# An attention recurrence and a feed-forward layer on one core: every on-chip transpose moved from the DMA crossbar to TensorE, in a newly searched order

## The chip, the core and the metric

The kernel runs on one core of a Trainium2 chip. A core has a matrix engine (TensorE, PE in the profile; its weight loads are listed apart as PEld), a vector engine (VectorE, DVE), a scalar engine (ScalarE, ACT), a general engine (GpSimd, POOL) and a queue engine (SyncE, SP) that here issues nearly all DMAs. Each engine takes its instructions strictly in the order in which the program gives them; engines wait for each other by semaphores. The metric is device microseconds (us) of one launch, median of several.

## What is computed

An RWKV-like linear attention over 768 steps, then a feed-forward layer with a squared ReLU:

```python
for t in range(S):                        # B, H, S, D = 4, 8, 768, 48
    cur = einsum('bhd,bhe->bhde', u * kt, vt)
    y[:, :, t] = einsum('bhd,bhde->bhe', rt, state + cur)
    state = wt[..., None] * state + einsum('bhd,bhe->bhde', kt, vt)
x = y.transpose(0, 2, 1, 3).reshape(3072, 384)
r = maximum(x @ w_in, 0)                  # w_in 384 x 2048
out = (s * r * r + b) @ w_out             # w_out 2048 x 384
```

## The kernel before

The recurrence is done in chunks of 128 steps: 6 chunks for each of 4 batches, 24 chunk-batches, numbered n = 0 to 23. The first four (`n < PK`, PK = 4) are handled as two interleaved pairs ("packed"). For one chunk-batch all 8 heads stand side by side, 384 numbers for each of 128 time steps. Its steps, by the names that the order uses:

- `load`: w, r, k, v come in by four DMAs (192 KB each); `ln`, `cum`, `exp`, `inc`, `exn`: the logarithm of w, its running sum (a matmul with a triangle), and the two exponentials E.
- `mul` (L482, L489, DVE): R and K times E give `prd`, bf16, two heads to a 128-wide block padded to 64 each: 8 blocks.
- `tr` (L538, TensorE): 8 matmuls against an identity turn the 8 blocks of `prd` into PSUM; `tev` (ACT L552 or DVE L554, by a mark in the order) copies them to the tile `RK`. For a chunk-batch that `xbar_rk(n)` names, `tev` is one DMA instead (L575, `dtrans`): the crossbar of the DMA turns `prd` into `RK`, with no `tr`.
- `mt` (L605, L617): 16 matmuls on `RK` for each chunk-batch, always two chunk-batches together; `msk` (L629, DVE): the masks; `ymm` (L667, L676): y from the state and from the masked products; `rkp`, `rku`, `yd`, `st` (POOL L346, L352, L375, L793) and `cd` (DVE): the diagonal term and the new state; `dmm`, `sup`: the state's increment.
- `yev` (L758): y goes to `x_sb`. `xtr` (L804, TensorE): 3 matmuls against an identity turn it, and `xev` (L552 or L554) copies that to `xT`. Where `xbar_x(n)` holds, `xev` is one crossbar DMA (L585, `dxtr`), with no `xtr`.

The feed-forward layer takes tiles T = 0 to 11 of two chunk-batches (256 rows). For each there are eight `g1` steps (L858: 6 matmuls of 128x256 each, into one PSUM bank), a `relu` (ACT L871) and a `sq` (square; ACT L881 or DVE L883) after each, then eight `g2` steps (L901: 4 matmuls of 128x384 each), `oev` (L912, DVE) and `store`. The weights are loaded and cast in five pieces (`li`/`lo`, `ci`/`co`).

What runs when is neither a loop nor a scheduler's choice at build time: the string `ORDER` lists all steps, one word each, and the kernel emits their instructions in that order; `@A`, `@D`, `@P` put a movable step on ACT, DVE or POOL, and `+3` emits three matmuls on a zero tile (L1286), which only fill TensorE. Since every engine takes its instructions in program order, the order of the words is the order on each engine and on SP's queue. The `Plan` that checks the words also holds the buffer rings: 6 PSUM banks of tag `P` and 2 of tag `o`, 4 `RK` tiles, 4 `rh` tiles. The costs and due times that its steps carry play no part when the kernel is built from the string.

The choice of the transposing unit is in these constants and lines:

```python
DTK = 9
DTX = 18
    def xbar_rk(n):
        return n >= DTK or (n >= DK2 and n % 2 == 1)
    def xbar_x(n):
        return n >= DTX or (n >= DX2 and n % 2 == 1)
```

So before the change 9 chunk-batches have R and K turned by TensorE and 15 by the crossbar, and 18 have x turned by TensorE and 6 by the crossbar.

Of the kernel before, what the change touches and what calls it, by code (L numbers as in the profile page):

```python
# [42 lines left out]
rkp0 mul0.0 load2.1 cum1.1 mul0.1 exp1.1 rkp1 load4.0 u_ev@D tr0 mul1.0 +4 tev0@A mul1.1 rku1 li0
tr1 load2.3 exl0 +2 rku0 cd1 tev1@A li1 ln2 cd0 mt0 load4.1 msk1.0 cum2.0 rkp3 l21 li2 msk0.0 +2 yd1
ln4 exp2.0 cum3.0 cum3.1 msk0.1 l20 rku3 ci0@A load4.2 msk1.1 cum4.0 +3 vb0@D vb1@A yd0 mul2.0
exp2.1 lo0 dmm0 exp3.1 mul2.1 +2 li3 exp3.0 li4 exl2 mul3.0 exp4.0 l23 cum4.1 sup0 vb3@P ymm0.0
exp4.1 tr2 rkp2 ci1@A mul3.1 st0 ymm0.1 sup1 ydm0 vb2@A l24 lo1 rku2 ymi0 yev0@D tr3 yev1@A tev2@D
xtr0 tev3@A xtr1 l22 +1 st1 xev0@D cd2 xev1@A mt2 cd3 rkp4 ci2@A g10.0 msk3.0 yd3 g10.1 msk2.0
relu0.0 lo2 msk2.1 yd2 ymm2.0 relu0.1 g10.2 msk3.1 rku4 dmm2 mul4 relu0.2 ymm2.1 ydm2 co0@A ci3@P
g10.3 sq0.1@A sup2 yev2@A cd4 st2 ymi2 sq0.2@A xtr2 sup3 yev3@A csred0@D lo3 g10.4 sq0.0@A ci4@D  # L50
load5.0 xev2@A xtr3 g10.5 load6.0 relu0.3 co1@D xev3@A lo4 g10.6 csred1@D sq0.3@A load5.1 g11.0
relu0.6 csadd1@D g11.1 relu0.4 co2@D relu0.5 g20.0 csred2@D sq0.4@A g10.7 sq0.6@A g11.2 sq0.5@A
relu0.7 g11.3 csadd2@D relu1.0 load5.2 g20.1 co3@D relu1.3 g20.4 relu1.1 load6.1 csred3@D ln5 g20.5
ln6 tr4 sq0.7@A cum6.0 csadd3@P tev4@D cum5.0 relu1.2 g11.4 inc6 sq1.3@A load6.2 g11.5 sq1.0@A co4@D
cum5.1 exp5.0 g11.6 small2 csred4@D exp5.1 load5.3 exp6.0 g20.6 exn6 g11.7 relu1.6 mul5 relu1.4
small g20.7 sq1.1@A load4.3 csadd4@D g20.2 relu1.7 load7.0 cssplit tr5 sq1.2@A load8.0 relu1.5 mul6
csspread g20.3 csevac load8.1 tev5@D vb5@P tr6 sq1.5@A rkp5 oev0.0 tev6@A mt4 load9.0 oev0.1 g21.4
l25 msk4.0 sq1.4@A rku5 load7.1 dmm5 g21.0 vb4@A msk5.0 g21.5 ln7 load7.2 sup5 rkp6 sq1.7@A msk4.1
cum7.0 st5 yd4 dmm4 load8.2 g21.1 load9.1 ln8 exp7.0 sup4 l26 cum8.0 cd5 st4 ymm4 ln9 msk5.1 yd5
g21.6 sq1.6@A inc7 load6.3 ymm5 exp8.0 st3 yev4 cum9.0 exn7 g21.7 yev5 rku6 inc8 xtr4 xtr5 g21.2  # L60
xev4@A load10.0 mul7 l27 xev5@A g21.3 exn8 load9.2 inc9 rkp7 g12.0 oev1.1 exp9.0 load9.3 g12.1 mul8
relu2.0 l28 relu2.1 load7.3 g12.2 cd6 l29 sq2.1@A sq2.0@D yd6 g12.3 load11.0 tr7 load10.1 exn9
oev1.0 relu2.2 g12.4 tev7@D vb6@P relu2.3 load8.3 g12.5 relu2.4 sq2.3@D mul9 sq2.4@A mt6 relu2.5
g22.4 msk7.0 store0.0 sq2.2@A vb7@P g12.6 msk6.0 sq2.5@A rkp9 load11.1 tev9 msk6.1 dmm6 g22.0
relu2.6 rku7 ln10 sup6 g12.7 load10.2 ln11 msk7.1 tr8 rku9 relu2.7 cd7 g22.1 sq2.7@A cum10.0 cd9
tev8@A load12.1 vb9@A dmm7 ymm6 rkp8 inc10 g22.5 rku8 yev6 load12.0 cum11.0 sup7 g22.6 yd9 xtr6
inc11 exp11.0 exp10.0 g22.2 yd7 xev6@A cd8 load15.0 ymm7 sq2.6@A vb8@P mt8 yev7 exn11 load13.0 st6
g22.3 exn10 msk8.0 st7 store0.1 xtr7 g22.7 xev7@D load11.2 msk8.1 rkp10 dmm9 load10.3 g13.0 store1.1
msk9.0 l210 g13.1 rku10 msk9.1 relu3.0 load11.3 g13.2 sq3.0@A sup9 yd8 mul10 g13.3 relu3.2 load12.2
st9 g13.4 ln12 relu3.1 g13.5 oev2.0 sq3.1@A ymm9 oev2.1 relu3.3 dmm8 g13.6 mul11 rkp11 relu3.4 rku11  # L70
sq3.3@A g13.7 load14.0 load13.1 sq3.2@A g23.0 sup8 relu3.5 g23.4 yev9 relu3.6 sq3.4@D l211 tev11
load13.2 sq3.5@A ymm8 cum12.0 relu3.7 yev8 xtr9 vb11@P g23.1 st8 ln13 inc12 tev10 xtr8 sq3.7@D g23.5
xev8@A exp12.0 g23.6 xev9@D store1.0 exn12 vb10@D load12.3 sq3.6@D cum13.0 ln14 dmm11 mul12 g14.0
exp13.0 ln15 g14.1 inc13 tev12 cd10 g23.2 exn13 cd11 load14.1 relu4.1 yd10 dmm10 g14.2 sup10 rkp13
g23.3 sup11 relu4.2 load14.2 mul13 g14.3 sq4.1@A rkp12 relu4.0 g14.4 oev3.0 relu4.3 tev13 mt10
sq4.0@A rku13 g23.7 relu4.4 load15.1 msk10.0 sq4.3@A g14.5 msk10.1 l213 sq4.2@A l212 rku12 msk11.0
cum14.0 g14.6 relu4.5 msk11.1 load13.3 exp14.0 st10 cum15.0 exp15.0 g14.7 oev3.1 vb12@A ymm11 inc15
load17.0 relu4.7 yd11 ymm10 sq4.4@D sq4.5@A g24.4 store2.0 st11 relu4.6 sq4.7@A g24.0 cd12 load16.0
inc14 load15.2 exn14 sq4.6@A rkp14 g24.5 yd12 cd13 mt12 yev10 load16.1 vb13@A rku14 yev11 g24.1
msk12.0 g24.6 msk12.1 store2.1 xtr10 xtr11 load19.1 msk13.0 g24.2 xev10@A xev11@A msk13.1 dmm12 ln16  # L80
g24.7 exn15 cd14 load16.2 g15.0 rkp15 mul14 g15.1 relu5.0 l215 g15.2 relu5.1 load19.2 sup12 g15.3
sq5.0@A mul15 dmm13 st12 relu5.2 ymm12 g24.3 relu5.3 load14.3 sup13 sq5.3@A oev4.1 g15.4 rku15
sq5.2@A yev12 g15.5 ln17 tev15 sq5.1@D yd13 tev14 relu5.4 ymm13 g15.6 oev4.0 cd15 load15.3 st13
cum17.0 relu5.6 xtr12 g15.7 xev12@D relu5.5 rkp16 yev13 g25.4 sq5.4@A load17.1 inc17 sq5.6@A l214
load18.0 g25.0 cum16.0 rku16 relu5.7 inc16 store3.0 xtr13 vb14@A rkp19 g25.5 xev13@D store3.1
exp17.0 exp16.0 g25.1 load17.2 l217 sq5.5@A rku19 load18.1 g16.0 load17.3 dmm14 yd15 g16.1 relu6.0
sup14 exn16 cd16 yd14 relu6.1 mt14 exn17 g25.6 msk14.0 load19.0 vb15@A g16.2 msk14.1 sq5.7@A
load16.3 mul16 g16.3 rkp17 sq6.0@A relu6.2 g16.4 msk15.0 g25.2 msk15.1 sq6.1@A relu6.3 load18.2
rku17 ln18 g16.5 sq6.3@A mul17 g16.6 tev16 st14 sq6.2@A dmm15 relu6.6 load20.3 cum18.0 ymm14 sup15
relu6.4 g25.7 cd19 l216 tev17 relu6.5 g25.3 vb16@P oev5.1 ln19 st15 g16.7 oev5.0 load20.0 rkp18  # L90
ymm15 exp18.0 vb17@D relu6.7 g26.0 yev14 sq6.4@A load21.0 inc18 rku18 cum19.0 xtr14 yev15 exn18
g26.4 inc19 xev14@A l218 g26.5 store4.1 sq6.5@A load22.0 sq6.7@A xtr15 dmm17 g26.1 load20.1 xev15@D
exp19.0 mul18 sq6.6@A g17.0 load18.3 exn19 sup17 dmm16 g17.1 relu7.0 sup16 cd17 g17.2 relu7.1
sq7.0@D g17.3 mul19 relu7.2 yd17 load19.3 g17.4 ln20 st17 relu7.3 mt16 load21.1 sq7.3@A g26.2
msk17.0 relu7.4 load20.2 ln21 st16 g26.3 msk16.0 sq7.2@A g17.5 msk17.1 yd16 store4.0 sq7.1@A
load21.2 msk16.1 cum21.0 g26.6 vb18@P tev19 oev6.0 ln22 l219 g17.6 vb19@P relu7.5 sq7.4@D inc21
store5.1 yd19 ymm17 relu7.6 tev18 ymm16 cum20.0 g27.4 yev16 rkp20 exp20.0 load23.0 yev17 exp21.0
g27.5 exn21 inc20 rku20 xtr16 sq7.5@D xtr17 g26.7 xev16@A load21.3 exn20 rkp21 dmm19 xev17@D g17.7
cd18 g18.0 sup19 relu7.7 rku21 mul20 store5.0 g18.1 sq7.7@A vb20@P yd18 cum22.0 g27.6 relu8.0 g18.2
oev6.1 tev20 exp22.0 mul21 relu8.1 load22.1 g18.3 sq7.6@A supn20 load22.2 relu8.2 g18.4 relu8.3  # L100
g27.0 inc22 sq8.0@A supn21 dmm18 cd20 mt18 sq8.1@D tev21 sup18 g27.7 relu8.4 msk19.0 sq8.3@A
load23.1 g27.1 msk18.0 ln23 g27.2 exn22 msk18.1 sq8.4@A g18.5 oev7.1 ymm18 rkp22 vb21@D sq8.2@A
g27.3 yev18 cum23.0 msk19.1 st18 xev18 g18.6 exp23.0 oev7.0 store6.0 yd20 g28.0 load23.2 inc23
relu8.6 ymm19 rku22 cd21 exn23 g18.7 relu8.5 g28.4 mul22 yd21 g28.5 relu8.7 sq8.5@A yev19 supn22
sq8.6@A mt20 sq8.7@D xev19 g28.1 load22.3 msk21.0 rkp23 load23.3 g28.6 msk20.0 tev22 g28.2 msk20.1
rku23 msk21.1 g28.7 st19 store6.1 mul23 g28.3 store7.1 ymm20 g19.0 cd22 supn23 tev23 ymm21 vb22@D
relu9.0 yd22 g19.1 yev20 sq9.0@A yev21 g19.2 xev20 relu9.1 sq9.1@A cd23 g19.3 oev8.1 yd23 g19.4
oev8.0 relu9.3 g19.5 store8.0 relu9.4 store8.1 g19.6 relu9.2 sq9.4@A g29.4 sq9.2@D relu9.5 xev21
g19.7 vb23@D sq9.3@A store7.0 sq9.5@A mt22 relu9.7 g29.5 msk22.0 relu9.6 g29.6 msk22.1 sq9.6@A g29.0
sq9.7@D msk23.0 g29.7 ymm22 g110.0 yev22 g110.1 msk23.1 xev22 oev9.1 g110.2 relu10.1 store9.1 g110.3  # L110
# [1216 lines left out]
```

## Time and profile before

| what | value |
|---|---|
| median of 3 runs | 183.34 us (183.16 to 183.92) |
| the profiled execution: its time | 183.5 us |
| its span, first to last instruction | 181.7 us |
| granted TensorE clock | 1.000 |
| DVE busy | 142.8 us (79%), 257 instructions |
| ACT busy | 142.2 us (78%), 279 instructions |
| POOL busy | 105.0 us (58%), 139 instructions |
| DMA queue of SP | 116,528 packets, 34.42 MB, 81.6% of 16 engines |
| crossbar DMAs `RK<-prd` | 15, 3.7 us from issue to landing |
| crossbar DMAs `xT<-x_sb` | 6, 2.6 us from issue to landing |

Busy is time in which an engine had at least one instruction running. Matmuls overlap in the pipeline, so the mean length of one (220 ns for a transposing matmul) is not the time by which it delays the next; that is seen from how many finish in a stretch. The chain of waits follows, from the last instruction backwards, what released each step, and lists stretches in order of time. The windows give busy time per engine in stretches of the span.

### The profile page before, as it was taken

To read this page: it belongs to the slowest core of one execution; us is meant where nothing else is said; L and a number is where in the kernel's file an instruction comes from. 1 tells how busy PE (TensorE), PEld (TensorE's weight loads), DVE (VectorE), ACT (ScalarE), POOL (GpSimd) and SP (SyncE) were. 2 spreads that over 40 slices of the span, in tenths; PEclk is the share of its full clock that TensorE was granted. 3 is DMA by queue.
4 is the path that set the end of the run, shared out by engine and by line. 5 is a ranking of instruction groups with operands and counts; after the bars stand their busy time and mean duration, and the time that the engine had idled before them with its cause. 6 is when DMAs were issued, how large, how long until landed. Compare 5 with 4: busy or idle time off the path is not lost.

```text
span 181.7 us, 4868 instructions
## 1 busy us (share of the span) xinstructions
PE 171.8 (95%) x1874; PEld 131.9 (73%) x1876; DVE 142.8 (79%) x257; ACT 142.2 (78%) x279; POOL 105.0 (58%) x139
## 2 busy tenths in 40 slices
...
GB/s 154 323 324 343 387 350 274 260 184 206 167 207 178 187 187 182 199 171 183 232 186 195 212 172 202 208 199 243 160 206 100 158 238 153 69 60 11 0 43 132
DMA packets 116554, 34.72 MB, mean 191 GB/s; under 512 B 110898, under 2 KB 114739, under 8 KB 116531
## 3 DMA queue, kind: packets, MB, share of 16 engines
q1 hardware_dynamic: 116528, 34.42, 81.6%
...
q10 hardware_dynamic: 2, 0.00, 0.0%
...
## 4 chain that ended last, share of the span: by engine, by line
PE 64%; DVE 10%; DMA 7%; POOL 6%; issue 5%; ACT 4%; SPq 1%; DVEq 0%; ACTq 0%; POOLq 0%
PE o_ps L901 27%; PE h_ps L858 26%; DMA wo_st<-in_moe_w_out_dram 4%; DMA rkt<-in_k_dram 3%; PE mt_ps L617 2%; POOL rkp L346 2%; PE y_ps L676 2%; DVE prd L489 2%; PE y_ps L667 2%; POOL rku L352 1%; POOL yd L375 1%; PE d_ps L741 1%; ACT rh L871 1%; PE cums L410 1%; PE xt_ps L804 1%
## 5 line engine op out<-in xcount | busy, mean ns | idle before, releaser
L901 PE MATMUL o_ps<-w_out,gT 128*128 128x384 bf16 (+2 forms) x400 | 71.8, 320 | 0.5 <-ACT gT L881 0.5
L858 PE MATMUL h_ps<-xT,w_in 128*128 128x256 bf16 x576 | 70.9, 273 | 1.1 <-POOL w_in L983 0.6
L871 ACT ACTIVATE rh<-h_ps 128x512 bf16<-128x512 f32 x96 | 54.4, 597 | 16.6 <-PE h_ps L858 15.7
L858 PEld LDWEIGHTS <-w_in 128*128 128x128 bf16 x576 | 59.9, 110 | 6.1 <-issue 1.0
L901 PEld LDWEIGHTS <-gT 128*128 128x128 bf16 x400 | 36.1, 98 | 19.7 <-ACT gT L881 0.7
L881 ACT ACTIVATE gT<-rh 128x512 bf16<-128x512 bf16 x78 | 47.4, 634 | 0.5
L352 POOL TENSOR_TENSOR rku<-rkp,u_bc 128x384 f32<-128x384 f32 x24 | 27.7, 1158 | 2.2 <-DVE cd L369 1.6
L346 POOL TENSOR_TENSOR rkp<-rkt 128x384 f32<-128x384 f32 x20 | 21.3, 1068 | 11.2 <-DMA rkt<-in_k_dram 9.4
L629 DVE TENSOR_TENSOR mt_sb<-mt_ps,tri_strict 128x512 bf16<-128x512 f32 x40 | 25.4, 681 | 1.9 <-PE mt_ps L617 1.8
L375 POOL TENSOR_TENSOR yd<-vt,cd 128x384 bf16<-128x384 f32 x20 | 17.6, 884 | 11.0 <-DVE cd L369 10.7
L489 DVE TENSOR_TENSOR prd<-rkt,E 128x768 bf16<-128x768 f32 x20 | 23.7, 1187 | 0.3 <-ACT E L473 0.3
L912 DVE SCALAR_TENSOR_TENSOR o_sb<-o_ps,s_bc,bconst 128x384 f32<-128x384 f32 (+2 forms) x25 | 14.6, 594 | 6.4 <-PE o_ps L901 6.3
L883 DVE TENSOR_TENSOR gT<-rh 128x512 bf16<-128x512 bf16 x18 | 9.6, 536 | 10.2 <-ACT rh L871 10.2
L793 POOL TENSOR_TENSOR st<-stmp,l 128x384 bf16<-128x384 bf16 x16 | 15.5, 972 | 0.8 <-DVE stmp L784 0.8
L758 DVE TENSOR_TENSOR x_sb<-y_ps,yd 128x384 bf16<-128x384 f32 x20 | 10.7, 549 | 5.3 <-PE y_ps L676 5.2
L369 DVE TENSOR_REDUCE cd<-rku 128x8 f32<-128x384 f32 x24 | 12.8, 542 | 1.4 <-POOL rku L352 1.4
L448 ACT ACTIVATE E<-cums 128x388 f32<-128x388 f32 (+1 forms) x22 | 10.4, 496 | 4.3 <-DVE inc L463 2.4
L784 DVE TENSOR_TENSOR stmp<-d_ps,st 128x384 bf16<-128x384 f32 x16 | 8.7, 550 | 3.2 <-PE d_ps L741 3.1
L473 ACT ACTIVATE E<-inc 128x384 f32<-128x384 f32 x18 | 9.3, 525 | 1.5 <-DVE inc L463 1.4
L1286 PE MATMUL warm_ps<-warm_sb 128*128 128x512 bf16 x22 | 7.7, 477 | 1.3 <-DVE warm_sb L1242 1.2
L983 POOL CAST vb<-vt 128x384 bf16<-128x384 f32 x9 | 5.6, 629 | 4.1 <-DMA vt<-in_v_dram 4.1
L676 PE MATMUL y_ps<-vb,mt_sb 128*128 128x48 bf16 x160 | 7.3, 183 | 0.0
...
## 6 DMA issues: line engine op xcount, KB each, us to landing
...
```

The lines of the kernel that those rows point to most:

```text
L346: nc.gpsimd.tensor_tensor(out=rkp, in0=c["r"], in1=c["k"], op=ALU.mult)
L352: nc.gpsimd.tensor_tensor(out=rku.rearrange("t h d -> t (h d)"), in0=c["rkp"].rearrange("t h d -> t (h d)"), in1=u_bc, op=ALU.mult,)
L369: nc.vector.reduce_sum(out=cd, in_=c["rku"], axis=AX.X)
L375: nc.gpsimd.tensor_tensor(out=yd, in0=c["v"], in1=c["cd"].unsqueeze(2).to_broadcast([128, H, D]), op=ALU.mult,)
L489: nc.vector.tensor_tensor(out=prd[:, :, :, 0:D], in0=c["rk"], in1=c["E"][:, :, 0:HD].rearrange("t x (h d) -> t x h d", h=H), op=ALU.mult,)
L629: nc.vector.tensor_tensor(out=c["mt"][:, sg], in0=c["mt_ps"][sg], in1=(masks[:, n % 2] if packed(n) else tri_strict) .unsqueeze(1) .to_bro ...
L793: nc.gpsimd.tensor_tensor(out=c["st_new"], in0=c["stmp"].rearrange("q p (g e) -> q p g e", g=2), in1=c["l2"].unsqueeze(3).to_broadcast([12 ...
L858: nc.tensor.matmul(ps[:, f, :], lhsT=w_in_sb[PIECE[ft]][:, kt, :].rearrange("p (m j) -> p j m", j=PIECES[PIECE[ft]])[:, ft - F0[PIECE[ft]] ...
L871: nc.scalar.activation(out=rh, in_=hs[T, i], func=AF.Relu)
L881: nc.scalar.activation(out=g, in_=rh, func=AF.Square)
L901: nc.tensor.matmul(os_[T, k][:, cols], lhsT=gT[T][:, ft, tt * 128 : (tt + 1) * 128], rhs=w_out_sb[PIECE[ft]][:, ft - F0[PIECE[ft]], cols], ...
L912: nc.vector.scalar_tensor_tensor(out=o_sb[:, cols], in0=os_.pop((T, k))[:, cols], scalar=s_bc, in1=bconst[:, cols], op0=ALU.mult, op1=ALU.add,
```

## The change

The thresholds are set above 23, so that no chunk-batch takes the crossbar: `tr` and `xtr` exist for all 24, and every `tev` and `xev` is a copy on ACT or DVE. `square` can now also emit on GpSimd. The string `ORDER` is replaced as a whole, by one that was searched anew (with the mean over randomly disturbed durations as its aim); with it movable steps change engine. Only the parts that are spoken of below are shown.

```diff
-DTK = 9
-DTX = 18
-DK2 = 24
-DX2 = 24
+DTK = 99
+DTX = 99
+DK2 = 99
+DX2 = 99
...
-load0.0 load0.2 +9 load0.1 ln0 load2.2 cum0.0 load0.3 cum1.0 exp0.0 +1 u_mm exp0.1 load2.0 exp1.0
...
+load0.0 load0.2 +9 load0.1 load2.0 ln0 load0.3 load2.1 cum0.0 cum1.0 rkp0 exp0.0 cum1.1 exp0.1 u_mm
...
+load17.0 store1.0 g22.7 rkp11 g13.6 sup9 oev2.1 relu3.5 sq3.1@A ymm8 rku11 load15.0 ymm9 relu3.6
...
+g18.4 sq8.0@D msk19.0 relu8.4 exn23 sq8.1@A g27.3 msk18.1 g27.7 tr21 oev7.1 g18.5 msk19.1 tev21@A
+tr22 g18.6 tev22@A oev7.0 mul23 ymm18 supn23 yev18 tr20 relu8.5 g18.7 sq8.3@A store7.0 relu8.6 ymm19
...
+xev22@A g210.0 xev23@A relu10.7 store9.1 g210.4 sq10.7@D sq10.5@P g111.0 g111.1 g111.2 relu11.1
+g111.3 relu11.0 sq11.1@D store8.1 sq11.0@P relu11.2 g111.4 g210.1 relu11.4 g210.2 relu11.3 sq11.3@D
+sq11.2@P g210.3 g111.5 relu11.5 g111.6 oev10.0 sq11.4@P g210.5 g111.7 sq11.5@P store10.0 g210.6
+relu11.7 relu11.6 g211.0 g211.1 g210.7 oev10.1 sq11.6@P g211.2 sq11.7@A g211.4 g211.3 g211.5 oev11.0
...
-            nc.vector.tensor_tensor(out=g, in0=rh, in1=rh, op=ALU.mult)
+            eng = nc.gpsimd if pl.ops["sq", T, i]["eng"] == "POOL" else nc.vector
+            eng.tensor_tensor(out=g, in0=rh, in1=rh, op=ALU.mult)
```

What it does to the instructions, counted in the two built programs:

| instructions | before | after |
|---|---|---|
| crossbar DMAs on SP (`RK`, `xT`) | 15, 6 | 0, 0 |
| transposing matmuls `trps`, each with its weight load | 72 | 192 |
| transposing matmuls `xt_ps`, each with its weight load | 54 | 72 |
| filling matmuls on the zero tile | 24 | 24 |
| copies to `RK`: ACT, DVE | 5, 4 | 11, 13 |
| copies to `xT`: ACT, DVE | 11, 7 | 10, 14 |
| squares: ACT, DVE, POOL | 78, 18, 0 | 61, 16, 19 |
| weight casts of 1536: ACT, DVE, POOL | 1, 4, 1 | 4, 1, 1 |
| weight casts of 768: ACT, DVE, POOL | 3, 1, 0 | 1, 1, 2 |
| casts of v: ACT, DVE, POOL | 8, 6, 10 | 9, 5, 10 |
| copy of u: ACT, DVE | 0, 1 | 1, 0 |

All other matmuls, loads and stores are the same in number and shape.

More of the change, by code (lines that the diff above doesn't have):

```diff
@@ L41 @@
 ORDER = """
-load0.0 load0.2 +9 load0.1 ln0 load2.2 cum0.0 load0.3 cum1.0 exp0.0 +1 u_mm exp0.1 load2.0 exp1.0
[L43 to L110, printed above, removed]
@@ L111 @@
-sq10.1@A g29.1 relu10.3 ymm23 sq10.3@A g110.4 relu10.0 yev23 g29.2 relu10.2 xev23 sq10.0@A g110.5
-relu10.4 g29.3 sq10.4@A g210.0 oev9.0 g110.6 sq10.2@D store9.0 g110.7 relu10.6 g210.4 relu10.5
-relu10.7 sq10.6@A g210.1 sq10.5@A g111.0 sq10.7@A g111.1 g111.2 relu11.1 g111.3 sq11.1@D relu11.2
-g111.4 relu11.0 g111.5 sq11.2@A g210.2 relu11.3 relu11.5 g111.6 sq11.0@A g111.7 sq11.3@A g210.5
-relu11.7 g210.3 relu11.4 sq11.7@D sq11.4@A g210.6 oev10.0 relu11.6 g211.4 sq11.5@D store10.0
-sq11.6@A g211.0 g211.1 g211.2 g211.5 g210.7 g211.3 oev10.1 g211.6 oev11.0 store10.1 g211.7 store11.0
@@ L117 @@
-g211.8 g211.9 oev11.1 g211.10 g211.11 store11.1 oev11.2 store11.2
+load0.0 load0.2 +9 load0.1 load2.0 ln0 load0.3 load2.1 cum0.0 cum1.0 rkp0 exp0.0 cum1.1 exp0.1 u_mm
+exp1.0 mul0.0 load2.2 +1 exp1.1 mul0.1 rkp1 u_ev@A li1 mul1.0 tr0 load4.0 load2.3 mul1.1 +3 tev0@A
+rku0 tr1 +3 exl0 vb0@A rku1 cd0 vb1@A li0 tev1@D ln2 yd0 mt0 load4.1 cum2.0 rkp3 msk1.0 +1 l20 rku3
+li2 msk0.0 cum3.0 ci1@A +1 rkp2 cd1 exp2.0 cum3.1 +1 msk0.1 li3 exp2.1 mul2.0 ln4 exp3.1 dmm0
+load4.2 exl2 msk1.1 +1 yd1 ymm0.0 exp3.0 mul2.1 ymm0.1 l22 ydm0 lo0 tr2 yev0@A rku2 sup0 l21 li4
@@ new lines @@
+vb3@A st0 ymi0 cum4.0 mul3.0 mul3.1 yev1@A l23 cum4.1 +1 ci0@P exp4.0 tr3 sup1 +3 tev2@A exp4.1 cd2
+lo1 st1 vb2@P ci2@A xtr1 cd3 xtr0 tev3@D xev0@D l24 mt2 yd3 xev1@D g10.0 msk2.0 yd2 lo2 msk2.1 g10.1
+load5.0 ci3@A msk3.0 load6.0 g10.2 msk3.1 rkp4 dmm2 relu0.0 lo3 sq0.0@A sup2 rku4 g10.3 st2 g10.4
+co0@D relu0.2 ymm2.0 sq0.2@A relu0.1 ymm2.1 ydm2 mul4 relu0.3 ymi2 sup3 yev2@A ci4@P cd4 yev3@D
+sq0.3@A relu0.4 g10.5 xtr2 sq0.1@A xev2@D xtr3 tr4 xev3@D relu0.5 co1@P sq0.5@A lo4 g10.6 relu0.6
+tev4@D load5.1 csred1@D g10.7 co2@A st3 csred0@D load5.2 load6.1 g11.0 g11.1 ln5 g20.0 sq0.4@D g11.2
@@ new lines @@
+ln6 relu1.0 relu0.7 csadd1@D csred2@D g20.1 sq0.7@A cum5.1 cum6.0 g20.4 relu1.2 sq0.6@A inc6
+csadd2@P g11.3 co3@D exp6.0 relu1.1 co4@A l26 g20.5 cum5.0 csred3@D g11.4 load6.2 g20.2 csadd3@D
+small load5.3 exp5.0 g20.3 g11.5 small2 exp5.1 sq1.1@A csred4@D g20.6 load4.3 sq1.2@A mul5 sq1.0@A
+g11.6 relu1.3 load8.0 exn6 csadd4@D relu1.6 tr5 cssplit g20.7 load7.0 relu1.5 relu1.4 mul6 csspread
+load9.0 g11.7 load7.1 sq1.5@P csevac tev5@D tr6 load8.1 sq1.3@A oev0.0 mt4 tev6@A oev0.1 yd4 sq1.4@A
+load7.2 g21.4 relu1.7 msk5.0 msk5.1 g21.5 load10.0 msk4.0 rkp5 g21.0 vb4@A rkp6 rku5 load8.2 ln7
@@ new lines @@
+g21.6 msk4.1 vb5@A dmm4 sq1.7@A cum7.0 sup4 dmm5 g21.1 ln8 inc7 st4 l25 sq1.6@A load9.1 load6.3 rku6
+ymm4 cd5 exp7.0 cum8.0 sup5 g21.2 exn7 load9.2 yd5 yev4 st5 ln9 mul7 exp8.0 l27 ymm5 g21.7 xtr4
+cum9.0 yev5 load10.1 rkp7 tr7 inc8 load7.3 xev4@A exp9.0 xtr5 g21.3 xev5@D rkp8 cd6 g12.0 inc9 exn8
+tev7@A rku7 g12.1 oev1.1 relu2.0 load8.3 mul8 g12.2 load11.0 relu2.1 rku8 sq2.1@A mt6 relu2.2
+sq2.0@A g12.3 msk6.0 g12.4 load11.1 cd7 rkp9 g12.5 relu2.3 msk6.1 g22.0 load12.1 vb6@P oev1.0
+relu2.4 ln10 msk7.0 vb7@P sq2.3@A rku9 exn9 msk7.1 load10.2 g12.6 relu2.5 l28 dmm7 g22.4 mul9
@@ new lines @@
+load11.2 sq2.2@A yd6 cd9 yd7 cum10.0 g12.7 store0.1 load12.3 ln11 load9.3 relu2.6 g22.1 inc10
+sq2.6@A sup7 exp10.0 sq2.5@A cum11.0 load12.0 cd8 relu2.7 inc11 dmm6 sq2.7@A g22.5 load10.3 exn10
+sup6 sq2.4@P tr9 tr8 l29 tev8@D ymm7 ymm6 vb8@P exp11.0 st7 yev7 load13.3 tev9@A g22.6 yev6 rkp10
+g22.2 mul10 exn11 xtr6 xtr7 st6 mt8 msk9.0 xev6@A xev7@A load13.0 g22.3 msk8.0 g13.0 msk8.1 store0.0
+load14.0 relu3.0 yd9 load14.1 yd8 msk9.1 g13.1 g13.2 vb9@P dmm8 ln12 load12.2 g13.3 relu3.2 sup8
+relu3.1 l210 tr10 mul11 sq3.2@P sq3.0@A g13.4 relu3.3 tev10@D oev2.0 g13.5 ln13 relu3.4 dmm9 sq3.3@A
@@ new lines @@
+load17.0 store1.0 g22.7 rkp11 g13.6 sup9 oev2.1 relu3.5 sq3.1@A ymm8 rku11 load15.0 ymm9 relu3.6
+g13.7 yev9 rku10 cum12.0 yev8 relu3.7 cum13.0 cd11 load11.3 rkp12 exp12.0 cd10 g23.4 xtr8 sq3.4@A
+load13.1 inc12 xtr9 load13.2 st9 vb10@D tr11 xev8@A g23.0 xev9@D l211 sq3.6@A exn12 st8 inc13 mul12
+g23.1 load14.2 exp13.0 dmm10 load14.3 rku12 g14.0 sq3.5@A store1.1 g14.1 relu4.0 load16.0 tev11@D
+sup10 l212 g14.2 relu4.1 yd10 cd12 tr12 vb11@D load16.1 g23.5 exn13 relu4.2 g14.3 tev12@D ln14
+sq3.7@A load15.1 sq4.0@D ln15 rkp13 rkp14 dmm11 mt10 sup11 relu4.3 g23.6 msk10.0 sq4.1@A rku13
@@ new lines @@
+load16.2 sq4.2@A sq4.3@A yd12 g14.4 msk10.1 g14.5 load19.1 st11 vb12@A msk11.0 msk11.1 mul13 g23.7
+yd11 relu4.5 g14.6 relu4.4 cum14.0 load18.3 ymm10 inc14 load15.2 ymm11 relu4.6 vb14@D cum15.0
+load16.3 tr13 exp14.0 st10 yev11 l213 ln16 yev10 sq4.6@A load15.3 g23.2 rkp16 exp15.0 oev3.1 exn14
+g14.7 load17.1 g23.3 sq4.5@P ln17 xtr11 load17.2 xtr10 oev3.0 g24.4 xev10@A vb13@P inc15 tev13@A
+g24.0 load18.1 rku14 xev11@A mul14 dmm12 g24.1 relu4.7 rkp15 vb16@A g15.0 relu5.0 load18.2 sq4.7@A
+store3.0 cd13 mt12 load21.1 sup12 sq5.0@A g24.5 rku16 g15.1 yd13 sq4.4@A store3.1 msk12.0 msk13.0
@@ new lines @@
+load18.0 g15.2 msk12.1 relu5.1 cd14 g15.3 msk13.1 load21.0 rku15 sq5.1@A relu5.2 l215 dmm13 cum16.0
+exn15 g24.2 sup13 store2.0 l214 g24.6 relu5.3 inc16 store2.1 cd16 tr14 load19.0 rkp17 exp16.0 vb15@P
+mul15 ymm12 exn16 load22.0 rkp18 yev12 g15.4 tev14@A g15.5 load17.3 load21.2 vb18@D sq5.3@A ymm13
+mul16 cd15 relu5.5 tr15 sq5.2@A rku17 relu5.4 g24.7 g15.6 xtr12 oev4.1 load20.1 tev15@A yev13
+sq5.4@A xev12@D yd14 g24.3 load22.3 relu5.6 cum17.0 st12 g15.7 load20.0 xtr13 ln18 rku18 oev4.0
+xev13@D exp17.0 inc17 dmm14 sq5.5@A g25.4 ln19 relu5.7 yd15 tr16 sq5.7@A g16.0 tev16@D st13 g16.1
@@ new lines @@
+yd16 load23.1 sq5.6@D g25.5 load20.3 relu6.1 load23.2 sup14 l216 exn17 load22.1 g16.2 load23.0 cd18
+g16.3 st14 relu6.2 mul17 g16.4 sq6.1@A relu6.0 rkp21 relu6.4 relu6.3 g25.0 cd17 mt14 g25.6 g25.7
+load19.2 store4.1 l217 dmm15 msk14.0 sq6.2@A sq6.0@A cum18.0 sq6.3@A msk14.1 vb17@P exp18.0 yd18
+ln20 load20.2 msk15.0 g16.5 sup15 ymm14 msk15.1 relu6.5 sq6.4@D load22.2 st15 inc18 g25.1 store4.0
+rkp23 dmm16 yev14 cum19.0 rku21 exn18 load21.3 g25.2 sup16 g16.6 load19.3 sq6.5@A g25.3 inc19 oev5.1
+mul18 xtr14 g16.7 cd21 exp19.0 st16 load23.3 ln21 tr17 relu6.6 sq6.6@P exn19 ymm15 tev17@A dmm17
@@ new lines @@
+g26.0 yev15 oev5.0 relu6.7 g26.1 xev14@D rku23 store5.0 xtr15 g26.2 xev15@D store5.1 sup17 g17.0
+mul19 rkp20 cd23 g17.1 relu7.0 rkp19 g17.2 relu7.1 mt16 cum20.0 relu7.2 msk17.0 msk17.1 sq6.7@A l218
+g26.4 rku20 msk16.0 msk16.1 g26.3 ln22 yd17 sq7.2@A l219 sq7.0@A g17.3 inc20 g26.5 rkp22 relu7.3
+g17.4 vb21@A oev6.0 rku19 exp20.0 ymm17 relu7.4 store6.0 ymm16 sq7.1@A yev17 cum22.0 dmm18 cd19
+g17.5 yev16 g26.6 g17.6 inc22 sq7.3@P yd23 cum21.0 exn20 cd20 mul20 exp22.0 sq7.4@A xtr16 g27.0
+vb22@A relu7.5 g26.7 sup18 g27.1 vb19@P supn20 exn22 inc21 yd19 relu7.6 xtr17 oev6.1 tr18 xev16@A
@@ new lines @@
+exp21.0 store6.1 xev17@A g17.7 tev18@D sq7.5@D tr19 yd20 st18 exn21 relu7.7 g18.0 tev19@D g27.4
+dmm19 st17 mul21 relu8.0 sq7.6@D g18.1 g18.2 relu8.1 supn21 mul22 g18.3 sq7.7@D sup19 ln23 relu8.2
+supn22 g27.2 st19 cum23.0 relu8.3 g27.5 sq8.2@D rku22 exp23.0 mt18 vb20@D inc23 g27.6 msk18.0 yd21
+g18.4 sq8.0@D msk19.0 relu8.4 exn23 sq8.1@A g27.3 msk18.1 g27.7 tr21 oev7.1 g18.5 msk19.1 tev21@A
+tr22 g18.6 tev22@A oev7.0 mul23 ymm18 supn23 yev18 tr20 relu8.5 g18.7 sq8.3@A store7.0 relu8.6 ymm19
+xtr18 tev20@D sq8.4@A g28.0 yev19 relu8.7 g28.1 sq8.5@A sq8.7@P xev18@D mt20 sq8.6@A tr23 msk21.0
```

8 lines of the change are left out of this document (added).

## The prediction

> **What bounds the kernel now.** I read the busy shares, then the windows, then the chain of waits from its end, then the groups of the steps that move. Busy time alone does not tell whether TensorE is at its pace, since its matmuls overlap.
>
> ```profile
> PE 171.8 (95%) x1874; PEld 131.9 (73%) x1876; DVE 142.8 (79%) x257; ACT 142.2 (78%) x279; POOL 105.0 (58%) x139
> ```
>
> ```profile
> 10.00:20.00 10.00, 8.16 (x172) 5.33 (x170) 9.27 (x18) 9.14 (x18) 8.77 (x15) 1.00 1.12 345
> 70.00:80.00 10.00, 10.00 (x115) 8.16 (x114) 8.44 (x18) 9.40 (x20) 5.52 (x7) 1.00 0.93 182
> 100.00:110.00 10.00, 10.00 (x101) 7.90 (x99) 6.75 (x12) 9.53 (x21) 7.09 (x9) 1.00 0.90 195
> 160.00:170.00 10.00, 10.00 (x83) 8.53 (x82) 1.37 (x3) 8.66 (x18) 0.00 (x0) 1.00 0.11 32
> ```
>
> Columns: the stretch and its length, then busy us of PE, PEld, DVE, ACT, POOL, granted clock, DMA share, GB/s. From 70 us on TensorE is busy 10.0 of 10 us at clock 1.00, while DVE, ACT and POOL change from stretch to stretch. The chain says that this is work at pace and not waiting that looks busy:
>
> ```profile
> 59.46 0.45 PE trps L538 x8
> ...
> 62.23 0.46 DVE x_sb L758
> 62.69 0.47 DVE stmp L784
> 63.16 0.47 DVE inc L463
> ...
> 67.36 3.93 PE h_ps L858 x36
> ...
> 73.14 1.30 PE o_ps L901 x8
> ...
> 75.05 0.19 PE xt_ps L804 x3
> ```
>
> A matmul of 256 columns takes 3.93/36 = 0.109 us, one of 384 columns 1.30/8 = 0.163; the same figures return in every stretch of the chain to 178.6 us. Apart from two breaks (62.2 to 65.5 and 112.0 to 114.0 us, during which TensorE still had other work) the chain is TensorE's alone from 58.6 us on. I counted all matmuls at their own distances from start to start: real work 161.2 us. The span of 181.7 then splits into 5.2 before the first real matmul, 161.2 of work, 3.2 for the 15 filling matmuls after that point (0.215 each), 3.1 after the last matmul, and about 9.0 of waits. Of these some 5.5 lie before 26.5 us (first `h_ps` at 20.1) and some 3.5 after. So whatever is added to TensorE after 26.5 us is paid in full, unless it falls into the 3.5 us.
>
> **The change part by part.** The profiled execution took 183.5 us (span 181.7 and 1.8 around it), 0.16 above the median of 183.34.
>
> (1) Transposes on TensorE. Fifteen more `tr` of 8 matmuls, 0.45 us each by the chain's row, are 6.75; six more `xtr` of 3, between 0.17 (0.34 for a run of 6 at 91.0 us) and 0.19, are 1.0 to 1.1. Sum 7.8 us. All belong to chunk-batches 9 and later, and in the new order the first of them (`tr10`, `tr9`) come among tile 2's and 3's steps, inside the full stretch. What hides them would be idle time of TensorE: 3.5 us at most. I charge all 7.8.
>
> The trace's 72 transposing matmuls are listed at a mean of 220 ns, but 8 of them finish in 0.45 us: the mean is the length in the pipeline, 56 ns the pace.
>
> [...]
>
> (2) The copies that follow them, and what makes room.
>
> ```profile
> L552 ACT COPY RK<-trps 128x1024 bf16<-128x1024 bf16 x5 | 5.0, 1008 | 1.7 <-PE trps L538 1.7
> L554 DVE COPY RK<-trps 128x1024 bf16<-128x1024 bf16 x4 | 2.7, 684 | 0.4 <-PE trps L538 0.2
> L552 ACT COPY xT<-xt_ps 128x384 bf16<-128x384 bf16 x11 | 5.1, 482 | 1.8 <-PE xt_ps L804 1.7
> L554 DVE COPY xT<-xt_ps 128x384 bf16<-128x384 bf16 x7 | 2.5, 352 | 2.3 <-PE xt_ps L804 2.3
> L881 ACT ACTIVATE gT<-rh 128x512 bf16<-128x512 bf16 x78 | 47.4, 634 | 0.5
> L883 DVE TENSOR_TENSOR gT<-rh 128x512 bf16<-128x512 bf16 x18 | 9.6, 536 | 10.2 <-ACT rh L871 10.2
> L793 POOL TENSOR_TENSOR st<-stmp,l 128x384 bf16<-128x384 bf16 x16 | 15.5, 972 | 0.8 <-DVE stmp L784 0.8
> ```
>
> ACT: 6 more `RK` copies +6.0, one `xT` less -0.5, 17 squares less -10.8, weight casts +2.8 (three more of 1536 at 1.49, two fewer of 768 at 0.83), u and one v +1.0: -1.5. DVE: 9 `RK` +6.2, 7 `xT` +2.5, two squares less -1.1, casts -2.9 (three fewer of 1536 at 0.95), u and one v less -1.1: +3.6. So ACT stays near 141 us and DVE goes to 146 while the span grows to about 189: 75% and 77%. Their cover is TensorE itself. If it fails at a hand-over, `mt` of that pair waits on TensorE with `g1` and `g2` queued behind it, as at 64.3 to 65.5 us now (1.0 us).
>
> (3) Nineteen squares on POOL; no such row exists. Lower bound: the state update without DVE beside it took 0.83 us for 384 columns, so 1.1 for 512. Upper bound: the longest two-input POOL row, 1.82 for 384 columns, so 2.4. I take the mean of the state update, bf16 and two inputs like the square: 0.972 x 512/384 = 1.3. 19 x 1.3 plus two casts of 0.75 are 26 us: POOL 131 of 189, 69%. Twelve of the 19 stand in tiles 9 to 11, where POOL is empty now (0.00 busy from 150 us). The last, `sq11.6@P`, is due before `g211.3`; counted from the start of `g111.4`, 14 steps stand ahead of that step, 13 of 0.65 and one of 0.49, which are 8.9 us. POOL has six squares to do, the first free to start at about 0.6: done at 0.6 + 7.8 = 8.4. It just fits; at 2.4 each it would be 6.1 us late. In tiles 0 to 8 seven squares add 9 us to POOL's queue of `rkp`, `rku`, `yd`, `st`, and with `st` late the next `ymm` would be.
>
> POOL beside DVE is seen in the rows: DVE squares with no POOL work beside them took 0.42 us, those wholly beside it 0.75, at most 1.23; `prd` 0.95 and 1.23. If each POOL square lengthens one DVE step by 0.3, that is 5.7 us on DVE, which ends at 80%: hidden.
>
> [...]
>
> (4) 21 DMAs leave SP's queue. The path by crossbar (3.7 us to landing) becomes 0.45 + 0.7 to 1.0. This is worth nothing: no row of the waits shows TensorE waiting for a crossbar DMA. The freed share of the DMA engines matters before 40 us, where loads are waited for, and there no crossbar DMA runs. Zero.
>
> (5) The new order. What stands before the first `h_ps` is the same steps and the same 24 fills. `load2.0` moves up from the sixth load to the fourth, but `ln2` is not bound by it: ACT was busy to 11.1 us with two `RK` copies, and `ln2` follows at once. In the new order one of these goes to DVE (-1.0) but u (0.5) and two casts of v (0.5 each) come ahead of `ln2` (+1.5). On DVE the copy delays the masks by about 0.7. Bounds -1.5 to +1.5; I take 0. The 3.5 us of later waits are drawn anew: between -3.5 (all gone) and +5 (the late `sq11.6`, or ten `mt` pairs at 0.5). I take -0.5, since three of the stops are longer than 0.5 us and a new order will hit others.
>
> Sum: 183.5 + 7.8 + 0 - 0.5 = 190.8 for an execution like the profiled one, 190.6 for the median.
>
> **Rivals.** *Copies or POOL set the pace* (192 to 197, say 194.0). DVE and ACT stay above 8 of 10 us in many windows, and each `RK` now needs one of them on time; ten pairs at 0.35 us add 3.5. For it: the 1.0 us stop at 64 us with fewer copies than there will be. Against: between 120 and 140 us DVE is busy 9.2 to 9.4 of 10 us now, and TensorE still 10.0.
> *The order gains more than I grant* (186.5 to 189, say 188.0): all but 1 us of the later waits go. For it: most are a few single stops (0.9 at 41.4, 0.6 at 57.9, 1.0 at 64.3). Against: DVE and ACT are near-full there.
> *Faster* (182.6). One mechanism: the start. If the first `h_ps` came earlier by as much as all fill (3.2) and wait (5.5) there, 191.3 - 8.7 = 182.6. It decides only from 8 us earlier than 20.1, that is at 12 us, where the first pair's `mt` alone ends at 11.8 now. Nearly excluded.
> *The transposes stay on the crossbar*: the built program has none left. Excluded.
>
> **How the numbers follow.** Chances: forecast 0.61 (189.2 to 192), pace of copies or POOL 0.19, order gains more 0.15, faster 0.03, and 0.02 for an order that gains so much at the start that nothing can be told. What can be told from no change is 0.5% (0.9 us). So faster 0.03, same 0.02, slower 0.61 + 0.19 + 0.15 = 0.95. Range for 8 in 10: 187.5 to 194.2, which leaves out the far halves of the two side cases and the two small ones.
>
> **What would show it.** Right: the chain is again TensorE from about 60 us to the end with `trps` near 24 x 0.45 = 10.8 us, `o_ps` and `h_ps` at 0.163 and 0.109 each, and first `h_ps` near 20 us. Wrong: `trps` at another pace; waits of `mt_ps` or `o_ps` for `RK` or for `gT` from POOL above 3 us in sum; first `h_ps` before 18.5; POOL squares above 1.5 us.

## The result, and the profile after

The changed kernel takes 188.88 us (median of 3, 188.46 to 189.76) against 183.34: ratio 1.0303, 95% interval 1.0235 to 1.0371. The profiled execution is the one of 188.88, its span 187.1 (before: 181.7). In all that follows a median is over all executions of a kernel, while its ratio leaves out those over 1.5% above the fastest of the same kernel.

The page of the kernel after, busy time of each engine:

```profile
PE 179.3 (96%) x2014; PEld 139.3 (74%) x2014; DVE 147.0 (79%) x266; ACT 140.8 (75%) x270; POOL 124.4 (66%) x160
```

The windows of the kernel after (columns as in the prediction):

```profile
10.00:20.00 10.00, 8.40 (x173) 5.58 (x172) 9.28 (x19) 7.72 (x17) 10.00 (x16) 1.00 1.13 351
70.00:80.00 10.00, 10.00 (x133) 8.50 (x132) 9.53 (x19) 9.04 (x20) 7.88 (x11) 1.00 0.97 198
100.00:110.00 10.00, 10.00 (x108) 7.81 (x106) 8.28 (x17) 9.85 (x20) 9.00 (x12) 1.00 0.99 197
120.00:130.00 10.00, 10.00 (x115) 7.89 (x115) 8.58 (x16) 8.84 (x20) 9.64 (x12) 1.00 0.08 30
160.00:170.00 10.00, 10.00 (x98) 7.81 (x97) 3.79 (x8) 5.22 (x11) 4.12 (x4) 1.00 0.12 45
```

TensorE is busy 10.0 of 10 us in the same stretches as before, at clock 1.00, only for longer. New is the DMA share of 0.08 in the row from 120 us: the last load is issued at 116 us, where it was 143 us before.

The chain of waits of the kernel after (start, length, what):

```profile
82.65 1.50 POOL yd L376
...
88.51 0.91 ACT RK L553
89.43 0.39 ACT xT L553
89.86 0.81 PE h_ps L859 x6
...
95.68 0.45 PE trps L539 x8
...
103.12 1.31 PE h_ps L859 x12
...
111.12 0.65 PE o_ps L903 x4
```

Eight transposes end 0.45 us after they begin, as before, and `h_ps` and `o_ps` keep their 0.109 and 0.163. But the chain is TensorE's alone only from 89.9 us on (58.6 before). One stop of 0.26 us, from 89.6 to 89.9 us, for a copy to `xT`, is enough to send it back through the `RK` copies, POOL and the loads, although TensorE was busy 10.0 of 10 us from 50 to 80 us. So a chain tells what ended last at each stop and not how long the stop was.

The groups of the kernel after that answer to those shown before:

```profile
L539 PE MATMUL trps<-shift,prd 128*128 128x128 bf16 x192 | 14.7, 220 | 0.7 <-DVE prd L490 0.4 <-DVE prd L483 0.2
L553 ACT COPY RK<-trps 128x1024 bf16<-128x1024 bf16 x11 | 11.2, 1021 | 1.0 <-PE trps L539 0.9
L555 DVE COPY RK<-trps 128x1024 bf16<-128x1024 bf16 x13 | 8.9, 684 | 0.8 <-PE trps L539 0.6
L882 ACT ACTIVATE gT<-rh 128x512 bf16<-128x512 bf16 x61 | 37.8, 640 | 0.3
L885 POOL TENSOR_TENSOR gT<-rh 128x512 bf16<-128x512 bf16 x19 | 20.2, 1069 | 34.5 <-ACT rh L872 33.5 <-DMA wt<-in_w_dram 1.0
```

A square on POOL takes 1.07 us in the mean (1.03 to 1.39). No row of the waits has TensorE waiting for one.

To see where the time went I took three marks in each trace: the first `h_ps` of tile 0, the first of tile 2, and the end of the last matmul. "Waits" are the sum of all distances from one matmul's start to the next beyond what the first one takes; about 2 us of it after tile 2 starts are the switch into and out of the `mt` matmuls (0.10 us into a row of them and 0.14 out of it, in the traces before and after). This count comes out larger than the 9.0 us of the prediction, so only its differences between traces are read.

| trace | first `h_ps` | tile 2 | last matmul | tile 2 to end | waits up to the first `h_ps` | to tile 2 | to the end |
|---|---|---|---|---|---|---|---|
| before | 20.08 | 50.88 | 178.58 | 127.70 | 6.58 | 4.25 | 5.81 |
| after | 19.91 | 50.63 | 184.20 | 133.57 | 5.96 | 3.76 | 4.55 |

The last matmul ends 5.6 us later (the span 5.4): 7.8 of added transposes, less 2.4 of waits (16.64 before, 14.27 after, over all).

### The profile page after: what moved, and what is told of

Same layout as the page of the kernel before. It is cut to its first block, busy times and chain, and to the rows that moved or that the text cites. A ratio compares the mean times of both kernels' runs of the same rounds, so it can differ in the third digit from the quotient of the medians.

```text
span 187.1 us, 5151 instructions
## 1 busy us (share of the span) xinstructions
PE 179.3 (96%) x2014; PEld 139.3 (74%) x2014; DVE 147.0 (79%) x266; ACT 140.8 (75%) x270; POOL 124.4 (66%) x160
## 4 chain that ended last, share of the span: by engine, by line
PE 50%; DMA 17%; SPq 13%; ACT 10%; issue 3%; POOL 3%; DVE 2%; DVEq 0%; POOLq 0%
PE o_ps L903 21%; PE h_ps L859 20%; DMA rkt<-in_k_dram 7%; SPq L311 5%; DMA wo_st<-in_moe_w_out_dram 5%; SPq L319 4%; DMA wi_st<-in_moe_w_in_dram 4%; PE trps L539 2%; ACT rh L872 2%; ACT gT L882 2%; SPq L827 2%; DMA wt<-in_w_dram 2%; PE mt_ps L618 2%; ACT RK L553 1%; PE y_ps L677 1%
## 5 line engine op out<-in xcount | busy, mean ns | idle before, releaser
L859 PE MATMUL h_ps<-xT,w_in 128*128 128x256 bf16 x576 | 72.8, 273 | 0.1
L859 PEld LDWEIGHTS <-w_in 128*128 128x128 bf16 x576 | 59.7, 110 | 6.1 <-DVE xT L555 0.4
L903 PEld LDWEIGHTS <-gT 128*128 128x128 bf16 x400 | 36.1, 98 | 18.2 <-issue 1.0
L885 POOL TENSOR_TENSOR gT<-rh 128x512 bf16<-128x512 bf16 x19 | 20.2, 1069 | 34.5 <-ACT rh L872 33.5
L882 ACT ACTIVATE gT<-rh 128x512 bf16<-128x512 bf16 x61 | 37.8, 640 | 0.3
L353 POOL TENSOR_TENSOR rku<-rkp,u_bc 128x384 f32<-128x384 f32 x24 | 25.8, 1081 | 0.2
L347 POOL TENSOR_TENSOR rkp<-rkt 128x384 f32<-128x384 f32 x20 | 23.0, 1157 | 3.6 <-DMA rkt<-in_k_dram 3.5
L376 POOL TENSOR_TENSOR yd<-vt,cd 128x384 bf16<-128x384 f32 x20 | 19.9, 999 | 1.4 <-DMA vt<-in_v_dram 1.1
L794 POOL TENSOR_TENSOR st<-stmp,l 128x384 bf16<-128x384 bf16 x16 | 13.2, 825 | 6.3 <-DVE stmp L785 4.7
L539 PE MATMUL trps<-shift,prd 128*128 128x128 bf16 x192 | 14.7, 220 | 0.7 <-DVE prd L490 0.4
L539 PEld LDWEIGHTS <-prd 128*128 128x128 bf16 x192 | 12.0, 98 | 2.7 <-DVE prd L490 0.7
L553 ACT COPY RK<-trps 128x1024 bf16<-128x1024 bf16 x11 | 11.2, 1021 | 1.0 <-PE trps L539 0.9
```

What stands on the lines that cost most here:

```text
L347: nc.gpsimd.tensor_tensor(out=rkp, in0=c["r"], in1=c["k"], op=ALU.mult)
L353: nc.gpsimd.tensor_tensor(out=rku.rearrange("t h d -> t (h d)"), in0=c["rkp"].rearrange("t h d -> t (h d)"), in1=u_bc, op=ALU.mult,)
L376: nc.gpsimd.tensor_tensor(out=yd, in0=c["v"], in1=c["cd"].unsqueeze(2).to_broadcast([128, H, D]), op=ALU.mult,)
L539: nc.tensor.matmul(ps[:, x * HP + p, :], lhsT=c["prd"][:, x, 2 * p : 2 * p + 2, :].rearrange("t h d -> t (h d)"), rhs=identity, is_transpo ...
L859: nc.tensor.matmul(ps[:, f, :], lhsT=w_in_sb[PIECE[ft]][:, kt, :].rearrange("p (m j) -> p j m", j=PIECES[PIECE[ft]])[:, ft - F0[PIECE[ft]] ...
L882: nc.scalar.activation(out=g, in_=rh, func=AF.Square)
```

## The experiments

Each time stands beside the kernel before on the same chip, so the ratios are what is compared. The kernel after has 1.0303; 0.0055 of ratio is 1 us.

**More matmuls.** The transposes of chunk-batches 9 to 23 done twice:

```diff
-        for x in range(2):
+        for x in [0, 1] * (2 if n >= 9 else 1):
             for p in range(HP):
                 nc.tensor.matmul(
                     ps[:, x * HP + p, :],
```

> The changed kernel with the 8 transposing matmuls of chunk-batches 9 to 23 done twice into the same bank, 120 matmuls more, no copy more. Theory (every matmul in the full stretch is paid at 56 ns): 188.9 + 6.7 = 195.6 us, 195 to 196.5. Rival (TensorE has slack that the copies or POOL leave, so that more matmuls fall into waits): at most 192.

Measured: 195.65 us, ratio 1.0663 (1.0577 to 1.0750), 6.6 us above the kernel after by the ratios; tile 2 to the end 139.81, that is 6.24 more than 133.57. 120 matmuls at 0.056 are 6.7. Added work on TensorE is paid nearly in full, as the theory has it.

**Fewer matmuls.** Only R turned, K's place filled from R's in a copy of the same size and length (1.02 us on ACT, 0.68 on DVE); run twice, since the first profile was 2.5 us late at tile 2, up to where nothing differs:

```diff
-        for x in range(2):
+        for x in range(1 if n >= 9 else 2):
...
-        move(("tev", n), RK, c["trps"])
+        if n >= 9:
+            move(("tev", n), RK.rearrange("q (x p) t -> q x p t", x=2),
+                 c["trps"][:, 0:HP].unsqueeze(1).to_broadcast([128, 2, HP, 128]))
+        else:
+            move(("tev", n), RK, c["trps"])
```

> The changed kernel without the 4 transposing matmuls of K for chunk-batches 9 to 23 (60 matmuls; K's place in RK is filled by a second copy of R's in the same copy of the same size). Theory (TensorE's work is the time): 188.9 - 60 x 0.056 = 185.5 us, 185 to 186. Rival (a wait takes the place of what is removed): 187 to 189.

> The run with half the transposes and full copies once more, since its profile had lost 2.5 us before tile 2, where nothing was changed. Theory: the loss at the start was chance, and from tile 2 to the end it takes 131.5 again, so 186.5 to 187.3 in all. Rival (a wait takes the place of all that was removed): 188 to 189.

Measured: 188.39 and 187.68 us, ratios 1.0285 (1.0217 to 1.0353) and 1.0225 (1.0163 to 1.0286). Tile 2 is reached at 53.11 and 50.53 us; from there to the end it takes 131.53 and 132.12. Of the 3.4 us that leave TensorE, 2.0 and 1.5 are gained; waits in that stretch are 5.70 and 6.31 in place of 4.55. So the first expectation failed twice over, by chance at the start and by new waits; the second (131.5 to the end again) came within 0.6 us, which is also how far two traces of one kernel lie apart here. More is paid nearly in full, less is gained by about half.

**The copies.** Doubled:

```diff
-        move(("tev", n), RK, c["trps"])
+        for _ in range(2 if n >= 9 else 1):
+            move(("tev", n), RK, c["trps"])
```

and halved, once with all matmuls kept and once with half of them left out as above:

```diff
-        move(("tev", n), RK, c["trps"])
+        h = HP if n >= 9 else 2 * HP
+        move(("tev", n), RK[:, 0:h], c["trps"][:, 0:h])
         c["RT"] = RK[:, 0:HP, :]
-        c["KT"] = RK[:, HP : 2 * HP, :]
+        c["KT"] = RK[:, h - HP : h, :]
```

> The changed kernel with the copy to RK of chunk-batches 9 to 23 done twice: 15 copies more, 9 on ACT at about 1.0 and 6 to 8 on DVE at 0.68, some 13 us of work on the two engines together. Theory (they lie beside TensorE): 188.9 plus 0 to 2 us. Rival (the copies are near the bound): plus 4 or more, with waits of mt or o_ps.

> The changed kernel with all transposing matmuls, but only R's half of RK copied for chunk-batches 9 to 23 (K is read from R's half). Theory (TensorE sets the time; the copies stand right behind and take a part only of what leaves TensorE): 188.9 minus 0 to 1.0, of the 4.6 us of waits after tile 2 starts at most 1. Rival (the copies themselves hold the kernel now): minus 2 or more.

> The changed kernel with only R turned for chunk-batches 9 to 23: 60 transposing matmuls less, and the 15 copies half as large (K's place is read from R's). The run with half the transposes and full copies kept half of the removed work as new waits from tile 2 on. Theory (the copies on ACT and DVE stand right behind TensorE, so that only both together give the time back): from the first h_ps of tile 2 to the last matmul 133.6 - 3.4 = 130.2 us or less, in all about 185.3. Rival (the copies play no part; what TensorE gains goes into waits for other things): 131.5 and 187 again.

| run | median | ratio | tile 2 to end | waits in it |
|---|---|---|---|---|
| copies twice | 193.70 | 1.0598 (1.0549 to 1.0647) | 137.96 | 8.73 |
| copies half, matmuls all | 189.98 | 1.0345 (1.0289 to 1.0402) | 133.48 | 4.35 |
| copies half, matmuls half | 185.56 | 1.0137 (1.0099 to 1.0175) | 130.52 | 4.77 |

Half the copies alone give 0.1 us from tile 2 on, and by the ratios the time is 0.8 us longer, within the intervals: at their present size the copies are hidden. Half of both gives 3.05 of the 3.4 us. Twice the copies costs 4.4 us of some 13 added on two engines: the theory's 0 to 2 failed, and the rival's 4 or more came. The waits of TensorE that the profile lists after 50 us are then for `xT` on ACT (0.9), `RK` (0.6), `relu` (0.5) and `x_sb` (0.4 twice), so that most of them are for other steps of these engines that come late, and not for the doubled copy itself. So ACT and DVE are not the bound, but they stand right behind it: with half the matmuls, two traces with full copies take 1.0 and 1.6 us longer than the one with half copies.

**The squares on POOL** put back on ACT and DVE by turns, 19 words of the order:

```diff
-sq1.5@P ... sq2.4@P
+sq1.5@A ... sq2.4@D
```

> The changed kernel with its 19 squares on POOL put on ACT (10) and DVE (9) by turns, in the same places of the order. Theory (TensorE sets the pace and ACT and DVE have room): 188.9 plus 0 to 1 us. Rival (the room that POOL gave to ACT and DVE is what lets TensorE run without waits): 191 or more, with waits of o_ps for gT.

Measured: 189.56 us, ratio 1.0345 (1.0258 to 1.0432), which can't be told apart from the 1.0303 of the kernel after; tile 2 to the end 133.79, that is 0.2 us more. These squares neither cost nor give anything that can be measured.

**The old order with all transposes on TensorE:**

```diff
-DTK = 9
-DTX = 18
+DTK = 99
+DTX = 99
...
-tev12
+tr12 tev12@A
```

> The old order with all transposes on TensorE: each crossbar word replaced in its place by tr and a copy (ACT and DVE by turns), 25 other words slip back a little so that the PSUM ring holds; no squares on POOL. Theory (7.8 us are paid and the new order took back 2 of them): 183.3 + 7.8 plus some new waits, 191 to 194 us. Rival (the order and the squares on POOL are worth nothing, the transposes cost 5.5): 188.4 to 189.5.

Measured: 195.09 us, ratio 1.0589 (1.0485 to 1.0694), 5 us (give or take 2) above the kernel after, at the upper end of what the theory gave. The words were put in without a search, so the 5 us are what an order made for this set of steps is worth against one that is not, and no measure of the old search against the new.

**The crossbar back in the new order,** throughout, and only where the loads are over:

```diff
-DTK = 99
-DTX = 99
+DTK = 9
+DTX = 18
...
-... mul10 ... tr10 ... tev10@D ...
+... mul10 tev10 ...
```

> The new order, its places for squares, casts and loads, but R and K of chunk-batches 9 to 23 and x of 18 to 23 turned by the crossbar again, each such DMA at the first place in the order that the rings allow; 138 transposing matmuls and 21 copies go. Theory (TensorE is at its pace, so its added matmuls are paid in full, and the new order by itself is 2 us better than the old): 188.9 - 7.8 = 181.1 us, 180 to 182.3, that is 1 to 3 us under the kernel before. Rival (the new order gains only because the transposes are on TensorE and come sooner than a crossbar DMA with its 3.7 us): 183 to 187, with waits of mt for RK.

Measured: 203.26 us, ratio 1.1025 (1.0927 to 1.1124): the theory's 181 missed by 22 us, and the rival's 183 to 187 by 16. The waits of this kernel (engine, line, released by: total, times, longest):

```profile
POOL rkp L346 <- DMA rkt<-in_k_dram: 10.8, 6, 3.2
...
PEld L617 <- DMA RK<-prd: 3.9, 1, 3.9
PE mt_ps L617 <- DMA RK<-prd: 3.8, 1, 3.8
```

`mt` of chunk-batches 8 and 9 waits 3.8 us for its `RK`, and loads come late (the same wait of `rkp` is 3.5 us in the kernel after and 9.4 in the one before). The `prd` of that `RK` was written by 59.7 us; its DMA was issued on SP at 64.6, behind loads and stores, and landed at 68.6. So about 5 us went in the queue and 4 from issue to landing. On SP's queue one transposing DMA took up to 2.1 us before the next instruction, among loads that the new order issues as early as it can. Not all of the loss is the loads': 3.6 us of waits of `h_ps` for the crossbar's `xT` come at 160.8 and 171.3 us, after the last load. In this run the granted clock also fell to 0.50 for 6.8 us in and after that stop of `mt`; it is told in the last section.

Only from 18 on, and from 14 on (in the order the words change as above, from there on):

```diff
-DTK = 99
-DTX = 99
+DTK = 18
+DTX = 20
```

```diff
-DTK = 99
-DTX = 99
+DTK = 14
+DTX = 20
```

> The changed kernel and its order, but R and K of chunk-batches 18 to 23 and x of 20 to 23 by the crossbar again, each DMA at the first place that the rings allow. In the changed kernel all loads are issued by 117 us and the DMA engines are nearly idle from 120 us on, when these DMAs come. 60 transposing matmuls go: 6 x 0.45 + 4 x 0.18 = 3.4 us. Theory (what leaves TensorE in its full stretch is gained in full as long as SP's queue is not behind): 188.9 - 3.4 = 185.5, 185 to 186.3. Rival (the 2 to 4 us to landing turn into waits of mt or h_ps): 187 to 190.

> As the run with 18, but R and K from chunk-batch 14 on; the DMAs of 14 to 17 stand among the last loads on SP's queue. Theory that SP's queue is what spoiled the new order with the crossbar throughout: these four cost something by delay of the loads, between 183.7 (188.9 - 10 x 0.45 - 4 x 0.18, no delay) and 187. Rival (the crossbar as such is bad in this order, wherever it stands): above 188.9.

From 18 on: 187.71 us, ratio 1.0251 (1.0190 to 1.0311), tile 2 to the end 131.76: 1.8 of 3.4 us gained, 1.4 back in waits (5.99). From 14 on, with four DMAs among the last loads: 190.48, ratio 1.0416 (1.0367 to 1.0464), tile 2 to the end 134.93 with 10.89 of waits; the 5.2 us of removed work are lost and 1.4 more. The second lies in the range of its rival, that the crossbar is bad wherever it stands; the first speaks against that. Where the crossbar's DMA met the loads on SP's queue, it cost more than it saved, by the 1.4 us; behind them it gained about half (1.8 of 3.4), which is what leaving out matmuls gained without any DMA.

**Six more x by the crossbar in the old order**, each DMA right after `yev`:

```diff
-DTX = 18
+DTX = 12
...
-... yev12 ... xtr12 ... xev12@D
+... yev12 xev12 ...
```

> The kernel before, with x of chunk-batches 12 to 17 by the crossbar too, each DMA right after yev: 18 transposing matmuls and 6 copies less. Theory (TensorE's work is the time): 183.3 - 1.0 = 182.3 us. Rival (SP's queue is full there, loads and RK come late behind the new DMAs): 183.5 to 187.

Measured: 193.69 us, ratio 1.0570 (1.0539 to 1.0600): 10.5 us slower for 1.0 us less on TensorE, where the theory gave 182.3 and the rival at most 187. The timeline of SP in this kernel (start, length, what):

```profile
112.39 1.44 SPq L574 DMA_TRANSPOSE RK<-prd  x1
113.93 0.53 SPq L309 DMA_DIRECT2D vt<-in_v_dram  x1
114.56 2.47 SPq L574 DMA_TRANSPOSE RK<-prd  x1
117.08 1.30 SPq L309 DMA_DIRECT2D wt<-in_w_dram  x1
118.47 1.36 SPq L584 DMA_TRANSPOSE xT<-x_sb  x1
119.93 0.53 SPq L309 DMA_DIRECT2D wt<-in_w_dram  x1
120.56 1.21 SPq L584 DMA_TRANSPOSE xT<-x_sb  x1
```

and its waits:

```profile
PE h_ps L857 <- DMA xT<-x_sb: 10.5, 3, 5.9
```

TensorE is out of work at 117.6 us and gets `xT` at 123.5: `x_sb` was written at 115.0 and 115.9 us, but the two DMAs stand behind two transposes of `RK` and three loads, so that they are issued at 118.5 and 120.6 and land at 121.5 and 123.4. No version was found that beats the kernel before.

## Why the prediction was right, and where it was off

- *TensorE sets the time, and what is added is paid* (step 1): right. 192 transposes come at 0.45 us for eight, and doubling the 120 new ones of `RK` cost 6.2 us where 6.7 were added. The pace of 56 ns held with 192 of them as with 72.
- *ACT and DVE hide the copies* (step 2): right at this size, 140.8 and 147.0 us busy where 141 and 146 were worked out, and halving the copies gave 0.1 us. That they would have room to spare is not so: twice the copies cost 4.4 us. The rival of copies that set the pace was near, not far. The stop at 64.3 to 65.5 us before was read wrongly as a late hand-over to `mt`: there the trace has TensorE waiting 0.15 us for an exponential on ACT and 0.52 for a square on ACT, and nothing for `RK`.
- *Squares on POOL* (step 3): 1.07 us each in place of the 1.3 that I took, a little under the lower bound of 1.1; POOL is busy 124.4 us, not 131. The last one was not late. Putting them back changed nothing beyond 0.2 us. Five DVE squares wholly beside POOL work took 0.68 us in the mean (0.41 to 1.09), those with none beside them 0.42, so that the 0.3 for one step was near; but the 5.7 us that 19 such steps would have added on DVE did not come: it is busy 147.0 us where 146 were worked out without them.
- *21 DMAs less on SP are worth nothing* (step 4): what TensorE waits for was read rightly, but the step looked at the old order alone. The new order issues its last load 27 us earlier, and with the crossbar's DMAs back on that queue it loses 13 us to the kernel after, by the ratios. So the new order needs the crossbar's DMAs gone, at least from among the loads; how much of the 13 us is the queue and how much the time of these DMAs from issue to landing (4 us for the one followed above) was not taken apart. Whether the freed queue also made the 2.4 us of waits go away was not tried.
- *The order gives back 0.5 us* (step 5): mis-sized. The start was as I took it (first `h_ps` 0.17 us earlier, waits there 0.6 less), but waits over all fell by 2.4, and not 0.5. Three quarters of it came after the first `h_ps`: 0.5 up to tile 2 and 1.3 behind it, where I had held that a new order would stop elsewhere as long. This accounts for the distance from 190.6 to 188.9. It is one trace each, and two traces of one kernel differed by 0.6 us behind tile 2 and by 2.6 us before it (fewer matmuls, above): the 1.3 is twice the spread there, the rest lies within it. The result lies at the upper edge of the stretch of the rival, an order that gains more (186.5 to 189), and just under the forecast's own (189.2 to 192), though of the later waits far less than "all but 1 us" went. The term had bounds and no mechanism, so that the time fell into the range is owed to its width, and partly to luck.
- *What would show it*: `trps`, `h_ps` and `o_ps` kept their pace and `h_ps` began at 19.9. The chain from about 60 us on did not come; it begins at 89.9, for the reason given with it.
